# Layer one: the loads of keys, queries, values and of the RMS row stay where the program writes them on the load queue

## The chip, the cores and the metric

One core of one Trainium2 chip runs the whole kernel. The metric is the device time of one execution in microseconds (us). PE is TensorE (matmuls and transposes), DVE is VectorE, ACT is ScalarE, POOL is GpSimd; SP issues nearly all DMAs from one queue.

## What is computed

```python
scores = where(block_i >= block_j, q @ k.T / sqrt(64), -1e9)   # B=4, H=8, S=576, D=64, blocks of 64
x = softmax(scores) @ v                                        # -> 2304 tokens x 512
h = x @ w_in;  x = (h - tanh(h)) @ w_out                       # 512 -> 2048 -> 512   "layer one"
xn = x / sqrt(mean(x * x) + 1e-6) * rms_g
x = (silu(xn @ w_gate) * (xn @ w_val)) @ w_out2                # 512 -> 1536 -> 512   "layer two"
```

All in float32, each product being made of three matmuls on high and low parts.

## The kernel before

The tokens are cut into six groups of 384. **Layer one** is a loop of 96 steps, `for s in range(NSA)` (six groups times sixteen slices of the 2048 hidden columns). A step multiplies x by a slice of w_in (L776 to L778), forms h - tanh h (ACT L1038, DVE L1044, then high part `gh` on ACT L112 and low part `gl` on DVE L116) and multiplies by a slice of w_out (L809 to L811). The slices are read again for each group from DRAM copies `w1d_i` and `w1d_o` by DMAs at L745 and L755; in the first group they are made from the raw weights, which come through a ring of three staging buffers `st` (DMA L138, then ACT L149 and L151, DVE L152 and L153).

**Attention is woven into these steps.** It consists of 32 pairs, numbered p0 to p31 here (eight units of query rows, four head pairs each). A pair's keys and queries are loaded raw into `kr` and `qr`, its values into `vr` (or straight into `vp`). There are two buffers of each, so the load for pair n+2 waits until pair n has left its buffer. Pairs p4 to p11 are loaded by rows (L299, 192 KB each) and reordered by POOL at L240; pairs p12 to p31 are loaded by four DMAs each for `kr` and for `qr` in 128-byte pieces (L289), and DVE turns them by `L348 STREAM_TRANSPOSE kt<-kr` and L359 `qt<-qr`. From `kt` come the high part `kh` (ACT L112) and the low part `kl` (POOL L116), which PE multiplies (L513, L527). The probabilities `pt` go through DVE L552 or L547, ACT L554, DVE L563 and then POOL L568 or ACT L570, and PE turns them (L583); `pp` holds them turned, in high and low parts. The program calls for the loads of a pair (`load`) when it has written the preparation of the pair two places earlier.

**What sets the order.** PE's order is written by hand and is the same as the program's. In layer one the order of DVE, ACT, POOL and SP is chosen by a scheduler when the program is built, from its own simulated times; each engine then runs its list strictly in that order, and an instruction at the head of a list that waits holds up all behind it. `pin` (L102) wraps an instruction so that this scheduler may not place it ahead of the instruction which the program wrote just before it on the same engine. It adds no wait for that instruction's completion. From the start of layer two onward the lists of DVE, ACT and POOL are written by hand too.

Of the kernel before, what the change touches and what calls it, by code (L numbers as in the profile page):

```python
# [21 lines left out]
NT, DM, FF1, FF2 = 2304, 512, 2048, 1536  # L22
KD = DM // 128
TG = 384
# [79 lines left out]
def build(ctx, tc, q, k, v, w_in, w_out, w_gate, w_val, w_out2, rms_g, ident_in, out):  # L104
    nc = tc.nc
    pin = tc.keep_in_program_order
    PE, ACT, DVE, POOL, SP = nc.tensor, nc.scalar, nc.vector, nc.gpsimd, nc.sync
# [23 lines left out]
    g_bc = com.tile([128, DM], F32, name="g_bc")  # L131
# [64 lines left out]
    def first_loads():  # L196
        qn, kn, vn = (nat.tile([128, 3, H, D], F32, name=x) for x in ("qn", "kn", "vn"))

        def rows(o, src, p, eng=SP):
            for h in (2 * p, 2 * p + 1):  # L200
                eng.dma_start(out=o[:, :, h], in_=src[0, h, 0:TG, :].rearrange("(t p) d -> p t d", p=128))
        ACT.dma_start(out=ident, in_=ident_in)
        rows(kn, k, 0)
        rows(qn, q, 0, ACT)
        rows(kn, k, 1)
        rows(qn, q, 1)
        for p in range(H // 2):
            if p == 2:
                env["kq"] = kq_loads(units[1], 0)
            if p < 3:  # L210
                stage1(p)
            if p < 2:
                rows(kn, k, p + 2)
                rows(qn, q, p + 2)
            rows(vn, v, p)
        env["nat"] = (qn, kn, vn)
# [16 lines left out]
    def by_rows(u):  # L233
        return u.group in (1, 2)

    def reorder(name, src, eng):

        t = at.tile([128, S], F32, name=name, tag=name, bufs=1)
        r = src[0:96, 0:512].rearrange("p (h t d) -> p t h d", h=2, t=4)
        eng.tensor_copy(out=t[0:96, 0:512].rearrange("p (t h d) -> p t h d", h=2, t=4), in_=r)  # L240
        return t
# [43 lines left out]
    def load_kq(src, b, p, name, r0, r1):  # L285
        t = at.tile([128, S], F32, name=name, tag=name)
        for a in range(4):
            hh, dh = divmod(a, 2)
            SP.dma_start(out=t[32 * a:32 * a + 32, 0:r1 - r0].rearrange("r (t c) -> r t c", c=32),  # L289
                         in_=src[b, 2 * p + hh, r0:r1, 32 * dh:32 * dh + 32]  # L290
                         .rearrange("(t r) c -> r t c", r=32))
        return t

    def kq_loads(u, p):
        d = {}
        if by_rows(u):
            for name, src in (("kr", k), ("qr", q)):
                d[name] = at.tile([128, S], F32, name=name, tag=name)
                SP.dma_start(out=d[name][0:96, 0:512].rearrange("p (h r) -> p h r", h=2),  # L299
                             in_=src[u.b, 2 * p:2 * p + 2, 0:TG, :].rearrange("h (p t) d -> p h (t d)", t=4))  # L300
        elif u.group:
            d["kr"] = load_kq(k, u.b, p, "kr", 0, u.nk)
            d["qr"] = load_kq(q, u.b, p, "qr", u.q0, u.q1)
        return d

    def v_loads(u, p, d):
        b, W = u.b, u.nk
        if by_rows(u):
            d["kt"] = reorder("kt", d["kr"], POOL)
            d["qt"] = reorder("qt", d["qr"], POOL)  # L310
        if u.group == 0:
            d["v"] = lambda j, hh: env["nat"][2][:, j, 2 * p + hh, :]
            return
        if u.light:
            o = at.tile([128, 5, 2, 128], F32, name="vp", tag="vp")[:, :, :, 0:D]
            d["v"] = lambda j, hh: o[:, j, hh, :]
        else:
            o = d["vr"] = at.tile([128, 5, 2, D], F32, name="vr", tag="vr")
        nf, rem = divmod(W, 128)
        for hh in range(2):  # L320
            SP.dma_start(out=o[:, 0:nf, hh, :],
                         in_=v[b, 2 * p + hh, 0:nf * 128, :].rearrange("(j r) d -> r j d", r=128))
            if rem:
                SP.dma_start(out=o[0:rem, nf, hh, :], in_=v[b, 2 * p + hh, nf * 128:W, :])

    def values_prep(u, d):
        W, nb, vr = u.nk, u.nb, d["vr"]
# [47 lines left out]
    class Attn:  # L375
# [56 lines left out]
        def load(self):  # L432

            n = self.nextload
            if n < len(self.pairs):
                self.loads[n] = env.pop("kq") if n == H // 2 else kq_loads(*self.pairs[n])
            if 0 < n <= len(self.pairs):
                v_loads(*self.pairs[n - 1], self.loads[n - 1])
            self.nextload += 1
# [212 lines left out]
    with tc.manual_schedule(engines={PE.engine}):  # L652
# [339 lines left out]
        for s in range(NSA):  # L992
            g, j = divmod(s, J1)
# [21 lines left out]
                att.upto(base, goal, si / nslots)  # L1015

            if s == 8:
                SP.dma_start(out=g_bc, in_=rms_g.rearrange("(o d) -> o d", o=1).broadcast_to([128, DM]))
            if g == 0:
                conv_upto(max(2 * j + 3, EARLY + (2 * J1 - EARLY) * (2 * j + 1) // 28))  # L1020
            if 0 <= s - (J1 - 1 + KEPT - SPLIT) < 3:
# [14 lines left out]
            h = hs.pop(s)  # L1036
# [356 lines left out]
```

## Time and profile before

| what | us |
|---|---|
| median of three runs | 1009.46 (1009.27 to 1010.65) |
| the profiled execution, whole | 1010.68 |
| its span in the trace | 1008.6 |
| PE busy | 995.9 |
| DVE busy | 711.6 |
| ACT busy | 661.5 |
| POOL busy | 362.5 |

The span is the time from the first to the last instruction of the trace; the execution is 2.1 us longer. Busy times are sums over an engine's instructions, so an engine at 99% leaves little that can be removed but much that can be added.

### The profile page before, as it was taken

How to read it: one execution, taken by the hardware profiler on the slowest of the kernel's cores; microseconds unless marked ns; L12 is line 12 of the kernel's file. 1: busy time of each engine (PE TensorE's matmuls, PEld its weight loads, DVE VectorE, ACT ScalarE, POOL GpSimd, SP SyncE). 2: the span in 40 equal slices, each digit the busy share in tenths (PEclk: the TensorE clock that was granted, in tenths of full speed). 3: DMA queues.
4: the chain of work that ended last, by engine and by line, in shares of the span. 5: the costliest groups of instructions: out<-in, count | busy, mean ns of one | idle time of the engine just before them, and what ended most of it. 6: DMA issues, size and time to landing. Idle time of an engine off the chain costs nothing.

```text
span 1008.6 us, 18034 instructions
## 1 busy us (share of the span) xinstructions
PE 995.9 (99%) x5995; PEld 911.6 (90%) x5995; DVE 711.6 (71%) x1569; ACT 661.5 (66%) x1538; POOL 362.5 (36%) x538
## 2 busy tenths in 40 slices
PE   8999999999999999999999999999999999999998
PEld 5666889899988988988899889989999999999998
DVE  6878875876768676787757887966854458644565
ACT  7879988887888777788858775635732247412253
POOL 6422213332234343445334424575121470111710
PEclk9999999999999999999999999999999999999999
DMA  9899889874788699877879998987796757876664
GB/s 212 272 348 360 242 244 279 232 197 122 211 248 209 179 253 269 238 213 240 303 225 373 364 353 310 351 322 283 270 353 250 251 224 260 303 280 233 259 228 155
DMA packets 185419, 265.22 MB, mean 263 GB/s; under 512 B 109040, under 2 KB 150384, under 8 KB 178032
## 3 DMA queue, kind: packets, MB, share of 16 engines
q1 hardware_dynamic: 184240, 263.69, 80.0%
q8 instruction: 47, 0.77, 0.3%
q10 hardware_dynamic: 1088, 0.39, 0.1%
q14 instruction: 44, 0.36, 0.1%
HBM read 202.70 MB, written 61.34 MB: 262 GB/s over the span
## 4 chain that ended last, share of the span: by engine, by line
PE 81%; DVE 8%; ACT 6%; issue 2%; DMA 1%; POOL 1%; DVEq 0%; ACTq 0%; POOLq 0%
PE t L776 5%; PE gv L1126 5%; PE t L778 5%; PE t L777 5%; PE acc L809 5%; PE gv L1128 5%; PE gv L1127 5%; PE acc L811 5%; PE acc L810 5%; PE t L583 4%; PE t L513 4%; PE ga L1128 3%; PE ga L1126 3%; PE ga L1127 3%; PE ga L811 3%; PE ga L809 3%
## 5 line engine op out<-in xcount | busy, mean ns | idle before, releaser
L776 PE MATMUL t<-xh,w 128*128 128x384 f32 x384 | 138.8, 361 | 0.0
L778 PE MATMUL t<-xh,w 128*128 128x384 f32 x384 | 129.9, 338 | 0.1
L777 PE MATMUL t<-xl,w 128*128 128x384 f32 x384 | 129.2, 337 | 0.0
L1126 PE MATMUL gv<-xh,ws 128*128 128x384 f32 x330 | 110.9, 336 | 0.5 <-DVE vb L1179 0.5
L1128 PE MATMUL gv<-xh,ws 128*128 128x384 f32 x330 | 111.0, 336 | 0.2 <-DVE ws L116 0.2
L1127 PE MATMUL gv<-xl,ws 128*128 128x384 f32 x330 | 110.7, 335 | 0.0
L809 PE MATMUL acc<-w,gh 128*128 128x512 f32 x264 | 109.1, 413 | 0.4 <-ACT gh L112 0.4
L811 PE MATMUL acc<-w,gl 128*128 128x512 f32 x264 | 104.5, 396 | 0.1
L810 PE MATMUL acc<-w,gh 128*128 128x512 f32 x264 | 103.9, 394 | 0.0
L1183 POOL TENSOR_TENSOR g<-va,vb 128x384 f32<-128x384 f32 x36 | 37.4, 1038 | 162.7 <-ACT va L1182 162.7
L554 ACT ACTIVATE pt<-pt,stat 128x64 f32<-128x64 f32 (+2 forms) x144 | 81.2, 564 | 17.1 <-DVE pt L552 11.6
L776 PEld LDWEIGHTS t<-xh,w 128*128 128x128 f32 x384 | 72.2, 188 | 7.1 <-issue 3.7
L777 PEld LDWEIGHTS t<-xl,w 128*128 128x128 f32 x384 | 72.4, 189 | 1.9 <-issue 0.5
L778 PEld LDWEIGHTS t<-xh,w 128*128 128x128 f32 x384 | 72.0, 188 | 0.8 <-DVE w L116 0.8
L116 DVE TENSOR_TENSOR gl<-gt,gh 128x384 fp32r<-128x384 f32 x88 | 58.3, 663 | 20.1 <-ACT gh L112 19.6
L116 DVE TENSOR_TENSOR pp<-t,pp 128x512 fp32r<-128x512 f32 (+3 forms) x112 | 55.3, 508 | 23.3 <-ACT pp L112 22.8
L583 PE MATMUL t<-ident,pt 128*128 128x128 f32 x400 | 65.1, 274 | 3.5 <-POOL pt L568 2.0
L1044 DVE TENSOR_TENSOR gt<-t,gt 128x384 f32<-128x384 f32 x88 | 48.5, 551 | 25.3 <-ACT gt L1038 24.7
L583 PEld LDWEIGHTS t<-ident,pt 128*128 128x128 f32 x400 | 49.7, 140 | 17.5 <-POOL pt L568 5.6
L112 ACT ACTIVATE pp<-t 128x512 fp32r<-128x512 f32 (+5 forms) x144 | 60.4, 437 | 5.8 <-PE t L583 4.6
L1126 PEld LDWEIGHTS gv<-xh,ws 128*128 128x128 f32 x330 | 61.9, 188 | 1.3 <-DVE vb L1179 1.2
L1128 PEld LDWEIGHTS gv<-xh,ws 128*128 128x128 f32 x330 | 61.9, 188 | 0.6 <-DVE ws L116 0.6
(210 smaller groups left out, 2946.0 us busy)
## 6 DMA issues: line engine op xcount, KB each, us to landing
ws<-w2d SPq DMA_DIRECT2D x26, 1792.0 KB, 7.5
ws<-wod SPq DMA_DIRECT2D x21, 1536.0 KB, 6.2
w<-w1d_i SPq DMA_DIRECT2D x60, 512.0 KB, 5.0
w<-w1d_o SPq DMA_DIRECT2D x52, 512.0 KB, 5.1
w2d<-ws SPq DMA_DIRECT2D x10, 1792.0 KB, 8.4
st<-in_moe_w_out SPq DMA_DIRECT2D x28, 512.0 KB, 6.2
st<-in_moe_w_in SPq DMA_DIRECT2D x16, 512.0 KB, 6.6
w1d_i<-w SPq DMA_DIRECT2D x16, 512.0 KB, 5.7
```

Source lines behind the costliest of these rows:

```text
L116: eng.tensor_tensor(out=o, in0=full, in1=hi.bitcast(F32), op=ALU.subtract)
L554: ACT.activation(out=pt[:, 0:keys], in_=pt[:, 0:keys], func=AF.Exp, scale=-1.0, bias=least, accum_out=st[:, 8 + ti:9 + ti])
L583: PE.transpose(t[:, (j - a) * 128:(j - a + 1) * 128], pt[:, j * 128:(j + 1) * 128], ident)
L776: PE.matmul(h, lhsT=wh[:, c], rhs=xh[:, kk], start=(kk == 0), stop=False)
L777: PE.matmul(h, lhsT=wh[:, c], rhs=xl[:, kk], start=False, stop=False)
L778: PE.matmul(h, lhsT=wl[:, c], rhs=xh[:, kk], start=False, stop=(kk == KD - 1))
L809: PE.matmul(acc, lhsT=gh[:, c], rhs=wh, start=first, stop=False, skip_group_check=more)
L810: PE.matmul(acc, lhsT=gh[:, c], rhs=wl, start=False, stop=False, skip_group_check=more)
L811: PE.matmul(acc, lhsT=gl[:, c], rhs=wh, start=False, stop=last, skip_group_check=more)
L1126: PE.matmul(ps, lhsT=wh[:, c], rhs=xh[:, kk], start=(first and kk == 0), stop=False, skip_group_check=more)
L1127: PE.matmul(ps, lhsT=wh[:, c], rhs=xl[:, kk], start=False, stop=False, skip_group_check=more)
L1128: PE.matmul(ps, lhsT=wl[:, c], rhs=xh[:, kk], start=False, stop=(last and kk == nk - 1), skip_group_check=more)
```

## The change

The six `dma_start` calls of L289, L299, L321, L324 and L1018 (keys, queries, values, RMS row `g_bc`) are wrapped in `pin`. Sizes, addresses, queue and buffers stay.

```diff
@@ load_kq
-            SP.dma_start(out=t[32 * a:32 * a + 32, 0:r1 - r0].rearrange("r (t c) -> r t c", c=32),
+            pin(SP.dma_start(out=t[32 * a:32 * a + 32, 0:r1 - r0].rearrange("r (t c) -> r t c", c=32),
...
@@ kq_loads
-                SP.dma_start(out=d[name][0:96, 0:512].rearrange("p (h r) -> p h r", h=2),
+                pin(SP.dma_start(out=d[name][0:96, 0:512].rearrange("p (h r) -> p h r", h=2),
...
@@ v_loads
-            SP.dma_start(out=o[:, 0:nf, hh, :],
+            pin(SP.dma_start(out=o[:, 0:nf, hh, :],
...
-                SP.dma_start(out=o[0:rem, nf, hh, :], in_=v[b, 2 * p + hh, nf * 128:W, :])
+                pin(SP.dma_start(out=o[0:rem, nf, hh, :], in_=v[b, 2 * p + hh, nf * 128:W, :]))
...
@@ layer one, s == 8
-                SP.dma_start(out=g_bc, in_=rms_g.rearrange("(o d) -> o d", o=1).broadcast_to([128, DM]))
+                pin(SP.dma_start(out=g_bc, in_=rms_g.rearrange("(o d) -> o d", o=1).broadcast_to([128, DM])))
```

PE's list is the same in both programs. Those of SP, DVE, ACT and POOL differ from the start of layer one until the end of attention, and are the same behind it. (The numbers in the names below tell one buffer's use from the next.)

**First place: SP's list at the start.** `st_366` and `st_493` are raw weights for layer one; `kr_468`/`qr_470` and `kr_576`/`qr_578` belong to the first two pairs that are loaded by rows after the first; `vr_1214` and `vr_1491` are values, `g_bc` the RMS row. Before:

```order
L201 DMA vn_150<-in_v 128x3x64 x4
L299 DMA kr_468<-in_k 96x2x256
L299 DMA qr_470<-in_q 96x2x256
L321 DMA vp_476<-in_v 128x3x64 x2
L321 DMA vp_584<-in_v 128x3x64 x2
L321 DMA vr_1214<-in_v 128x3x64 x2
L1018 DMA g_bc_121<-in_moe2_rms_g 128x512
L321 DMA vr_1491<-in_v 128x3x64
L299 DMA kr_576<-in_k 96x2x256
L321 DMA vr_1491<-in_v 128x3x64
L138 DMA st_366<-in_moe_w_out 128x1024
L299 DMA qr_578<-in_q 96x2x256
```

And after:

```order
L201 DMA vn_150<-in_v 128x3x64 x4
L138 DMA st_366<-in_moe_w_out 128x1024
L299 DMA kr_468<-in_k 96x2x256
L299 DMA qr_470<-in_q 96x2x256
L321 DMA vp_476<-in_v 128x3x64 x2
L710 DMA w1d_i_0_85<-w100_356 128x1024
L138 DMA st_493<-in_moe_w_in 128x4x256
L299 DMA kr_576<-in_k 96x2x256
L299 DMA qr_578<-in_q 96x2x256
L321 DMA vp_584<-in_v 128x3x64 x2
```

The raw weights have moved ahead of `kr_468`; the values for later pairs and `g_bc` (five DMAs) have gone from this place to ones far behind it.

**Second place: SP's list around the keys of pair p27, `kr_5197`.** The rows L745 and L755 are weight slices of layer one. Before:

```order
L745 DMA w103_4774<-w1d_i_11_96 128x1024
L289 DMA kr_5197<-in_k 32x18x32 x4
L745 DMA w102_4841<-w1d_i_10_95 128x1024
L828 DMA x2d_63<-x2s_4715 128x512
L745 DMA w101_4910<-w1d_i_9_94 128x1024
L828 DMA x2d_63<-x2s_4761 128x512
L828 DMA x2d_63<-x2s_4769 128x512
L289 DMA qr_5202<-in_q 32x6x32 x4
L755 DMA w113_4776<-w1d_o_11_112 128x1024
```

And after:

```order
L755 DMA w113_5066<-w1d_o_7_108 128x1024
L890 DMA wod_84<-wc_5126 128x3x256 x2
L745 DMA w100_5285<-w1d_i_4_89 128x1024
L755 DMA w112_5137<-w1d_o_6_107 128x1024
L289 DMA kr_5197<-in_k 32x18x32 x4
L289 DMA qr_5202<-in_q 32x6x32 x4
L745 DMA w103_5364<-w1d_i_3_88 128x1024
L755 DMA w111_5235<-w1d_o_5_106 128x1024
```

The keys stood between slices 11 and 10 of a group and stand now between slices 4 and 3 of it, with the queries right behind them.

**Third place: DVE's list around the transposes of the same pair.** Before:

```order
L116 TENSOR_TENSOR gl_5093<-gt_5089,gh_5092 128x384
L348 STREAM_TRANSPOSE kt_5451<-kr_5197 128x576
L116 TENSOR_TENSOR pp_5068<-t_5139,pp_5068 128x4x128
L563 RECIPROCAL stat_4956<-stat_4956 128x3
```

And after:

```order
L116 TENSOR_TENSOR gl_5254<-gt_5250,gh_5253 128x384
L613 TENSOR_TENSOR avt_5275<-t_5268,avt_5275 64x384
L348 STREAM_TRANSPOSE kt_5451<-kr_5197 128x576
L359 STREAM_TRANSPOSE qt_5480<-qr_5202 128x192
L116 TENSOR_TENSOR wc_5359<-fu_4469,wc_5359 128x1024
L613 TENSOR_TENSOR avt_5295<-t_5289,avt_5295 64x384
L116 TENSOR_TENSOR pp_5308<-t_5309,pp_5308 128x4x128
```

`kt_5451` has moved fourteen rows back in the list, behind two more slices' `gl`, and both transposes now stand together.

## Rows read from the trace of the kernel before

**Rows 1.** The head of the page: span; busy time and instructions of each engine.

```profile
span 1008.6 us, 18034 instructions
PE 995.9 (99%) x5995; PEld 911.6 (90%) x5995; DVE 711.6 (71%) x1569; ACT 661.5 (66%) x1538; POOL 362.5 (36%) x538
```

**Rows 2.** Busy time by stretch: PE, PEld, DVE, ACT, POOL; PE clock, DMA share, GB/s.

```profile
0.00:40.00 40.00, 35.79 (x222) 24.62 (x224) 30.48 (x118) 29.82 (x103) 25.73 (x68) 1.00 0.93 234
40.00:100.00 60.00, 58.74 (x284) 41.56 (x285) 47.90 (x112) 52.46 (x130) 14.02 (x29) 1.00 1.00 339
100.00:500.00 400.00, 398.33 (x2295) 355.72 (x2294) 296.57 (x752) 328.44 (x795) 142.77 (x254) 1.00 0.81 231
```

**Rows 3.** PE's waits over the whole span: us in total, times, longest us.

```profile
PE t L583 <- POOL pt L568: 2.0, 3, 1.3
...
PE t L583 <- DVE xs L623: 0.9, 1, 0.9
...
PE t L583 <- DVE gt L1044: 0.5, 1, 0.5
...
PE t L527 <- DVE pp L116: 0.3, 1, 0.3
```

**Rows 4.** DMA issues of the whole span: times, KB each, median us from issue to landing.

```profile
kr<-in_k SPq DMA_DIRECT2D x64, 72.0 KB, 4.5
...
qr<-in_q SPq DMA_DIRECT2D x64, 24.0 KB, 3.5
```

**Rows 5.** Line L348: its instructions (ns min/median/max), and all that DVE waited for.

```profile
L348 DVE STREAM_TRANSPOSE kt<-kr x20: 536/769/779, 145.1 to 447.5; 128x576 f32<-128x576 f32 x16, 128x384 f32<-128x384 f32 x4
...
  POOL kl L116: 2.5, 3
```

**Rows 6.** SP's timeline at the start: start us, us, instruction.

```profile
16.96 1.56 SPq L299 DMA_DIRECT2D kr<-in_k  x1
...
24.36 0.48 SPq L1018 DMA_DIRECT2D g_bc<-in_moe_rms_g  x1
...
26.99 0.38 SPq L299 DMA_DIRECT2D qr<-in_q  x1
```

**Rows 7.** Line L299 from 26.9 to 27.3 us, one load: from issue to landing.

```profile
DMA to landing us min/median/max: 6.4/6.4/6.4
```

**Rows 8.** POOL's timeline at the start: start, us, instruction, idle time ahead in brackets.

```profile
33.53 0.61 POOL L240 COPY qt<-qr 96x512 f32<-96x512 f32 x1 [3.26 <-PE t L513]
```

**Rows 9.** The chain of waits from 30 to 66 us: start us, us, what.

```profile
34.12 0.65 POOL pt L568
...
54.59 6.30 DMA st<-in_moe_w_out
```

**Rows 10.** SP's timeline around 384 us, one row.

```profile
384.44 0.44 SPq L755 DMA_DIRECT2D w<-w1d_o  x1
```

**Rows 11.** Line L289 from 95 to 480 us: issues (ns min/median/max), and issue to landing.

```profile
L289 SPq DMA_DIRECT2D kr<-in_k x80: 312/491/2447, 103.1 to 414.4; - x80
...
DMA to landing us min/median/max: 1.6/3.8/7.4
```

**Rows 12.** DVE's timeline from 376 to 394 us.

```profile
376.66 0.77 DVE L348 STREAM_TRANSPOSE kt<-kr 128x576 f32<-128x576 f32 x1
...
385.37 0.55 DVE L613 TENSOR_TENSOR avt<-t,avt 64x384 f32<-64x384 f32 x1
388.16 1.75 DVE L116 TENSOR_TENSOR wc<-fu,wc 128x1024 fp32r<-128x1024 f32 x1 [2.25 <-ACT wc L864]
...
392.59 0.78 DVE L348 STREAM_TRANSPOSE kt<-kr 128x576 f32<-128x576 f32 x1 [0.34 <-POOL kl L116]
...
393.73 0.68 DVE L116 TENSOR_TENSOR pp<-t,pp 128x512 fp32r<-128x512 f32 x1
```

**Rows 13.** PE's timeline, one row: the first matmul into the bank that this pp empties.

```profile
396.93 0.50 PE L527 MATMUL t<-kh,qp 64*128 64x512 f32 x2
```

**Rows 14.** The chain of waits from 100 to 480 us, one row.

```profile
376.74 0.69 DVE kt L348
```

More of the change, by code (lines that the diff above doesn't have):

```diff
@@ L288, in load_kq @@
             hh, dh = divmod(a, 2)
-            SP.dma_start(out=t[32 * a:32 * a + 32, 0:r1 - r0].rearrange("r (t c) -> r t c", c=32),
-                         in_=src[b, 2 * p + hh, r0:r1, 32 * dh:32 * dh + 32]
-                         .rearrange("(t r) c -> r t c", r=32))
+            pin(SP.dma_start(out=t[32 * a:32 * a + 32, 0:r1 - r0].rearrange("r (t c) -> r t c", c=32),
+                             in_=src[b, 2 * p + hh, r0:r1, 32 * dh:32 * dh + 32]
+                             .rearrange("(t r) c -> r t c", r=32)))
         return t
@@ L298, in kq_loads @@
                 d[name] = at.tile([128, S], F32, name=name, tag=name)
-                SP.dma_start(out=d[name][0:96, 0:512].rearrange("p (h r) -> p h r", h=2),
-                             in_=src[u.b, 2 * p:2 * p + 2, 0:TG, :].rearrange("h (p t) d -> p h (t d)", t=4))
+                pin(SP.dma_start(out=d[name][0:96, 0:512].rearrange("p (h r) -> p h r", h=2),
+                                 in_=src[u.b, 2 * p:2 * p + 2, 0:TG, :].rearrange("h (p t) d -> p h (t d)", t=4)))
         elif u.group:
@@ L320, in v_loads @@
         for hh in range(2):
-            SP.dma_start(out=o[:, 0:nf, hh, :],
-                         in_=v[b, 2 * p + hh, 0:nf * 128, :].rearrange("(j r) d -> r j d", r=128))
+            pin(SP.dma_start(out=o[:, 0:nf, hh, :],
+                             in_=v[b, 2 * p + hh, 0:nf * 128, :].rearrange("(j r) d -> r j d", r=128)))
             if rem:
-                SP.dma_start(out=o[0:rem, nf, hh, :], in_=v[b, 2 * p + hh, nf * 128:W, :])
+                pin(SP.dma_start(out=o[0:rem, nf, hh, :], in_=v[b, 2 * p + hh, nf * 128:W, :]))
     def values_prep(u, d):
```

## The prediction, written before the changed kernel was run

> **What bounds the kernel now.** I read the head of the page first. PE is busy for 995.9 of 1008.6 us [rows 1], so a change that leaves PE's list as it is can only add to or take from the 12.7 us in which PE idles. The busy time by stretch says where these lie: 4.2 us in the first 40 us, 1.3 from 40 to 100, and 1.7 in the 400 us in which attention and layer one run together [rows 2]. The lists behind attention do not change. So the change can win back at most about 7 us, part of which is the start that no load list shortens; 3 us (the middle two stretches) and the one start-up wait below are what is really in reach. What it can lose has no such bound. PE's waits name the releasers: POOL L568 for 2.0 us in three waits, all of them at the start, then single waits of 0.9, 0.5 and 0.3 us on DVE [rows 3]. No wait of PE in the middle names a DMA. Last I looked at L348, since its `kr` is what the change delays: in 20 transposes DVE idled ahead of them only for POOL, 2.5 us in three waits, and never for the load [rows 5].
>
> **The change, part by part.** `pin` adds no instruction and no byte. It moves DMAs on SP, and the scheduler rearranges DVE, ACT and POOL around them.
>
> *1. The start, gain.* POOL's copy `qt<-qr` at 33.53 us stood idle for 3.26 us [rows 8]. The row names PE, but the load that it reads was issued at 26.99 [rows 6] and took 6.4 us [rows 7], so it landed at 33.4: the load came last. Behind the copy in POOL's list stands L568 [rows 9], and behind that the longest of PE's waits on it, 1.3 us [rows 3]. In the new list five DMAs that stood ahead of this load are gone (four of 96 KB of values and the RMS row of 256 KB, 640 KB). At the 234 GB/s of this stretch [rows 2] they are 2.7 us of transfer. That is more than the 1.3 us that PE waited, so I take a gain of 1.3 us; bounds 0 and 1.3.
>
> *2. The start, loss.* 512 KB of raw weights now go ahead of `kr_468`, which was issued at 16.96 [rows 6]. By the same rate it lands 2.2 us later. No row tells how much of that PE would see; bounds 0 and 2.2, and I take 0.5, near the lower end, since the copies that need it are followed by 1.5 us and more of POOL idling in the same stretch (POOL is busy 25.7 of 40 us [rows 2]). What the raw weights gain by going first is bounded by the chain's one long DMA step there, 6.3 us for an `st` [rows 9]; PE idles only 1.3 us from 40 to 100, so this can return 0 to 1.3 us. I take nothing.
>
> *3. The middle, loss: DVE stands in front of the load.* Pair p27 shows it. Before, `kt<-kr` ran at 376.66 [rows 12], with its keys long there. In the new list the keys follow the load of `w112_5137`, which is the one at 384.44 [rows 10]. The four issues take 0.49 us each [rows 11], the last at 384.88 + 3 x 0.49 = 386.35, and land 4.5 us after it [rows 4], at 390.9. DVE comes to the transpose behind `avt`, which ends at 385.37 + 0.55 = 385.92 [rows 12]. It waits 4.9 us. After 0.77 for the transpose it is 391.6; the queries, issued behind the keys (last at 388.2, 3.5 us to landing [rows 4]), are there at 391.7, and 0.38 us later, at 392.1, DVE comes to `wc`, which ran at 388.16. Ahead of `wc` DVE had idled for 2.25 us anyway, which is counted in this: the list is 3.9 us late. What that costs PE: the row `pp` at 393.73 comes 3.9 us later, less the 0.78 + 0.34 of the next pair's transpose and its wait, which no longer stands ahead of it [rows 12]: at 396.5, ending at 397.2. PE's L527 writes into the bank that this empties at 396.93 [rows 13], so PE waits 0.3 us there. Other rows of that piece have less to spare: followed along the dependencies to the next matmul that needs them, I read 0.8 us where this one has 2.5, and that gives 2.0. I take 1.2 us for p27.
>
> I went through the other 19 transposes in the same way, with the new place in SP's list, 4.5 us to landing, and the new place in DVE's list. Seven (p27 among them) come out with DVE waiting 1.7 us or more, about 16 us in all; eight with 0.2 to 1.1 us, 4 us in all; five with none. DVE is busy 297 of 400 us here [rows 2], so a wait is soon made good, and DVE can slip by 0.9 to 3 us before PE notices. The eight small ones cost nothing. The six other large ones leave 0 to 1 us each; I take 0.4, so 2.4 us, and with p27 3.6. The bounds are 0 (all is covered) and 16 - 7 x 0.9 = 9.7 us (the least cover everywhere). I take a value in the lower half, nearer to the reckoned row than to the sum with least cover.
>
> What would cover go to? A late `kt` makes `kh` (ACT) and `kl` (POOL) late as well, but PE wants them later still: the L527 at 396.93 [rows 13] is still that of p26, and comes 6 us after the keys of p27 land by the reckoning above. So the loads alone are not late for PE; only what stands behind them in DVE's list is.
>
> *4. The middle, gain by the new order.* Where the transpose moves away from a tight spot, it frees it. The chain of waits has `kt` L348 in it at 376.74 for 0.69 us [rows 14], just ahead of the wait of 0.3 us that PE has on `pp` [rows 3]. I count 0.3. The waits of 0.9 and 0.5 us [rows 3] may vanish or grow with any new order; bounds plus and minus 1.4, taken as 0.
>
> *5. Stores and weight slices on SP.* The loads now come in one piece of 8 to 12 issues, 0.49 us each [rows 11], so up to 5 us in which no slice of w_in or w_out is issued. No wait of PE in the middle is put down to a slice [rows 3], and the slices are read three steps ahead. I count 0, bounds 0 and 1.
>
> The sum: -1.3 + 0.5 + 3.6 - 0.3 = +2.5 us. The profiled execution took 1010.68 us, 1.2 over the median of the three runs (1009.46). On the median's side that is 1012.0 us.
>
> The Trainium skill, DMA: Bandwidth & Descriptors, in its section Anatomy of one DMA, gives for a DMA of GpSimd's path a fixed 2.0 us plus the bytes at 436 GB/s. For 72 KB that would be an estimate of 2.2 us, where the row on this kernel's SP path has 4.5 [rows 4]. By the page's figure DVE would wait 2.3 us less at each large pair and step 3 would come to about zero, the sum to -0.9 us. I keep to the row.
>
> **The rivals.** *Quick landings or full cover: no change.* If the new, emptier queue lets the loads land near the shortest of 1.6 us [rows 11] rather than at 4.5, each of the seven waits shrinks by 2.9 us, from 16 to about 2 in all, and nothing reaches PE. Or the cover is just wider than I read. Then the steps 1, 2 and 4 are left: 1009.5 - 1.1 = 1008.4 us, within the limit. For it speaks that DVE idles a quarter of the time; against it that DVE's list runs strictly in order and some places have under 1 us.
>
> *Faster.* The start gains its 1.3 us, the staging ring passes on its 1.3, step 2 costs nothing, and the new order loses PE's waits in the middle (1.7): up to 4.3 us, 1005.2; I would expect 1006.5. For it speaks that 1.4 MB (the 640 KB of step 1 and 768 KB of keys and queries of p8 and p9) leave the stretches in which the DMA engines are busiest, at 0.93 and 1.00 [rows 2]. Against it, PE's waits of 40 us onward name engines and no load.
>
> *Much slower.* The cover is at its least everywhere, and the waits feed each other, since a late DVE makes PE late, PE frees the slices' buffers late, and SP, in order, issues the next keys later still. It decides from the point where a wait of DVE exceeds 0.9 us at most pairs: +9.7 + 0.5 - 1.6 = 1018 us.
>
> *It does not do what it says.* That would be an SP list unchanged, and the lists show otherwise: no chance given.
>
> **How the numbers follow.** A measurement of this kernel tells a difference of about 0.2%, 2 us, from no change. Slightly slower, +2 to +6 us: 0.35. Much slower, above +6: 0.08. Within 2 us: 0.30. Faster by over 2 us: 0.27. My forecast of 1012.0 stands close to the limit, so part of its chance is in the middle case already. The slower cases hold 0.43, the likeliest single one from 1011.5 to 1015.5. The range for 8 in 10 reaches down to 1006, most of the faster case, and up to 1017, most of the way to the much slower one.
>
> **What would show it.** Right: L348 of the new trace idles on a DMA `kr<-in_k`, some 10 to 20 us in all, with five to ten waits over 1.5 us; PE's waits between 100 and 500 us grow from 1.7 to about 5 us, on DVE `pp`, `pt` or `gt`; the wait of 1.3 us on POOL L568 is gone, and `qt<-qr` is copied about 1 to 3 us earlier. Wrong: L348 idles on DMA and PE's idle time in this stretch stays at 1.7 (cover was wider); L348 does not idle on it (landings were quicker); or PE's waits grow on ACT or on slices `w` (step 5). If the time drops under 1007.5, the start or the staging ring held more than PE's waits show.

## The result: 1.5% slower

The changed kernel takes 1023.68 us (median of five runs, 1023.18 to 1027.89) against 1009.46 before: a ratio of 1.0148, with a 95% interval of 1.0135 to 1.0161. Its profiled execution took 1023.68 us as well, with a span of 1021.8. The direction was forecast and the size was not: +14.2 us where +2.5 was predicted, outside the range.

The head of its page, then the busy time by stretch (PE, PEld, DVE, ACT, POOL; PE clock, DMA share, GB/s), which answer to [rows 1] and [rows 2]:

```profile
span 1021.8 us, 17998 instructions
PE 1000.4 (98%) x5995; PEld 913.7 (89%) x5995; DVE 715.6 (70%) x1569; ACT 659.5 (65%) x1538; POOL 363.3 (36%) x538
```

```profile
0.00:40.00 40.00, 37.10 (x232) 25.60 (x232) 30.25 (x118) 30.04 (x104) 23.59 (x67) 1.00 0.85 215
40.00:100.00 60.00, 58.18 (x277) 41.40 (x275) 48.20 (x109) 51.12 (x125) 17.04 (x33) 1.00 0.96 323
100.00:500.00 400.00, 389.32 (x2218) 345.04 (x2217) 290.70 (x734) 315.02 (x771) 136.96 (x246) 1.00 0.76 224
```

PE idles 2.9 us in the first 40 (4.2 before), and 10.7 us from 100 to 500 (1.7 before). So in these two traces the start is better and the middle much worse. Since PE's list is the same, the start of each matmul can be compared in the two traces, and the delay read off as it builds up (worked out from these starts):

| matmul starts, before | after | delay |
|---|---|---|
| 20.12 | 20.44 | +0.3 |
| 34.81 | 33.66 | -1.2 |
| 100.09 | 99.77 | -0.3 |
| 180.12 | 181.03 | +0.9 |
| 240.05 | 244.95 | +4.9 |
| 300.00 | 306.81 | +6.8 |
| 340.10 | 351.12 | +11.0 |
| 440.13 | 452.50 | +12.4 |
| 500.05 | 513.60 | +13.5 |
| 1000.02 | 1013.15 | +13.1 |

From 100 to 500 us PE loses 13.8 us; behind attention nothing is added and 0.4 us is given back. Where the loss comes from is shown by lines L348 and L359 of the changed kernel (first the transposes of keys, then those of queries; under each what DVE waited for: us, times):

```profile
L348 DVE STREAM_TRANSPOSE kt<-kr x20: 578/778/779, 159.1 to 474.8; 128x576 f32<-128x576 f32 x16, 128x384 f32<-128x384 f32 x4
...
  DMA kr<-in_k: 18.3, 14
  DMA qr<-in_q: 2.7, 1
```

```profile
L359 DVE STREAM_TRANSPOSE qt<-qr x20: 357/378/581, 160.4 to 475.9; 128x192 f32<-128x192 f32 x16, 128x384 f32<-128x384 f32 x4
...
  DMA qr<-in_q: 7.3, 9
```

Before, DVE never waited for a load there [rows 5]. Now it waits 28.3 us in 24 places. PE's waits (us in total, times, longest) have moved from POOL to what stands behind these transposes on DVE, where [rows 3] had 0.3 us on `pp`:

```profile
PE t L776 <- DVE gt L1044: 2.7, 2, 1.4
PE t L619 <- DVE pp L116: 2.2, 1, 2.2
PE t L527 <- DVE pp L116: 1.8, 2, 1.0
PE t L513 <- DVE pp L116: 1.5, 1, 1.5
```

How a load reaches PE stands in the chain of waits from 200 to 240 us (start us, us, what), around the loads of p16:

```profile
209.93 0.47 SPq L289
210.44 0.47 SPq L289
210.96 0.47 SPq L289
211.47 2.72 DMA qr<-in_q
...
214.31 0.59 DVE qt L359
214.92 0.52 ACT qh L112
215.47 0.52 ACT qh L112
216.01 0.87 ACT pt L554 x2
216.88 0.49 ACT pp L112
217.40 0.69 DVE pp L116
```

SP issues the eight loads of a pair one after the other, about 0.5 us each, the last one lands, DVE turns the queries, ACT splits them twice, and only then does ACT's list come to `pt` and `pp`, for which DVE and then PE wait. The late transpose is therefore passed on through two lists, DVE's and ACT's. At this one place, with 1.1 us of DVE waits (0.41 at L348 and 0.73 at L359), PE lost 2.4 us. They are not p16's alone: DVE had waited another 1.5 us for the loads of p15 only 8 us earlier.

The chain has a way back too, ahead of the loads of p17:

```profile
224.05 0.67 DVE w L116
224.74 0.32 SPq L751
225.11 0.42 SPq L289
```

In the new list these loads stand behind a store of layer one (L751), which waits for what DVE writes at L116, so here a late DVE makes the next loads late. SP idled ahead of L751 for DVE's `w` for 18.6 us in five places, against 2.1 us in two before.

At the start, POOL's timeline shows what the prediction expected, against [rows 8]:

```profile
31.22 0.61 POOL L240 COPY qt<-qr 96x512 f32<-96x512 f32 x1 [0.25 <-DMA qr<-in_q]
```

The copy comes 2.3 us earlier, and the matmul behind it gains 1.5 us between one start and the next. That the change brought this is not shown; e1 and x9 below speak against it.

### The profile page after: what moved, and what is told of

It is laid out like the page before. It is cut to its first block, busy times and chain, and to the rows that moved or that the text cites. A ratio compares the mean times of both kernels' runs of the same rounds, so it can differ in the third digit from the quotient of the medians.

```text
span 1021.8 us, 17998 instructions
## 1 busy us (share of the span) xinstructions
PE 1000.4 (98%) x5995; PEld 913.7 (89%) x5995; DVE 715.6 (70%) x1569; ACT 659.5 (65%) x1538; POOL 363.3 (36%) x538
## 4 chain that ended last, share of the span: by engine, by line
PE 61%; DVE 12%; ACT 11%; DMA 6%; SPq 4%; issue 4%; POOL 1%; DVEq 0%; ACTq 0%; POOLq 0%
PE gv L1126 5%; PE gv L1128 5%; PE gv L1127 5%; SPq L289 4%; PE acc L809 3%; PE t L776 3%; PE acc L811 3%; PE acc L810 3%; PE t L778 3%; PE t L777 3%; PE ga L1128 3%; PE ga L1126 3%; PE ga L1127 3%; PE ga L811 2%; PE ga L809 2%
## 5 line engine op out<-in xcount | busy, mean ns | idle before, releaser
L116 DVE TENSOR_TENSOR pp<-t,pp 128x512 fp32r<-128x512 f32 (+3 forms) x112 | 55.6, 510 | 23.5 <-ACT pp L112 22.9
L116 DVE TENSOR_TENSOR gl<-gt,gh 128x384 fp32r<-128x384 f32 x88 | 57.9, 658 | 19.2 <-ACT gh L112 19.0
L112 ACT ACTIVATE gh<-gt 128x384 fp32r<-128x384 f32 x88 | 45.8, 520 | 31.0 <-DVE gt L1044 30.5
L1126 PEld LDWEIGHTS gv<-xh,ws 128*128 128x128 f32 x330 | 61.9, 188 | 1.3 <-DVE vb L1179 1.1
```

What stands on the lines that cost most here:

```text
L112: return ACT.activation(out=o, in_=i, func=AF.Copy)
L116: eng.tensor_tensor(out=o, in0=full, in1=hi.bitcast(F32), op=ALU.subtract)
L1126: PE.matmul(ps, lhsT=wh[:, c], rhs=xh[:, kk], start=(first and kk == 0), stop=False, skip_group_check=more)
```

## The experiments

**Theory A**: DVE, which runs its list in order, stands in front of loads that land just behind it, and PE pays. **Theory B**: the scheduler's new lists for DVE, ACT and POOL cost time by themselves. **Theory C** came up with the result: A holds, but the time by which DVE may slip is smaller than the prediction reckoned.

The kernels named x hold the lists fixed. Each instruction of DVE, ACT, POOL and SP gets the edge that `pin` adds (issue order, no wait), from its predecessor in a table; so the lists are the changed kernel's row by row, except for what is said. Differences in time are against the kernel before on the same chip in the same series.

**One part alone.** First the change without L289, then L289 alone (the change wraps five calls in all, not six):

```diff
@@ e2_rest_only: load_kq as before, the other four calls pinned
-            pin(SP.dma_start(out=t[32 * a:32 * a + 32, 0:r1 - r0].rearrange("r (t c) -> r t c", c=32),
+            SP.dma_start(out=t[32 * a:32 * a + 32, 0:r1 - r0].rearrange("r (t c) -> r t c", c=32),
```

> The change for L299, L321, L324 and L1018 alone; the loads of L289 (keys and queries of p12 to p31) stay free for the scheduler. Theory A: L348 does not wait for its loads, as before; the start gains its 1.3 us; the time is 1007.5 to 1010 us. Theory B (any new order costs): DVE's list differs from the one before in 54 rows instead of 245, so part of the loss stays, 1011 to 1018 us.

> The change for L289 alone (keys and queries of p12 to p31); L299, L321, L324 and L1018 stay free. Theory A: the whole loss of the middle is here, without the gain of the start, 1020 to 1026 us. If the loads of values and of the RMS row carry part of the loss: 1012 to 1018 us.

The first took 1009.43 us against 1009.98, ratio 0.9995 (0.9986 to 1.0005): no change, and L348 waits for no load. The second took 1026.09 against 1009.77, ratio 1.0161 (1.0146 to 1.0176), just above its range, with 29.2 us of DVE waits on loads at the two lines. So the whole loss is in the loads of keys and queries of p12 to p31.

The gain of 1.5 us at 34 us appears in both; in the first it is used up by 53 us (+1.5 us at one matmul there). But the lists of e1 are those of the kernel before up to 105 us, and x9 below, which has the lists of before throughout, shows the gain as well. POOL's copy in x9:

```profile
31.79 0.61 POOL L240 COPY qt<-qr 96x512 f32<-96x512 f32 x1 [1.81 <-PE t L637]
```

In e1 it is at 32.07. Both issue its load at 25.5 us, where the profiled execution of before, which took 1.2 us more than the median, issued it at 26.99 [rows 6]. So the wait of 1.3 us at 34 us was that execution's own. At 100 us PE stands 0.3 us ahead of the trace of before in e1 and 0.9 in x9; in the kernels with all of the changed lists there it stands between 0.3 us behind and 2.1 us ahead, so one trace cannot tell what the start gains or loses. By e2's time the changes of the start are worth nothing that can be measured.

**The loads alone, earlier or later.** The lists of PE, DVE, ACT and POOL are the changed kernel's; on SP's list the eight loads of each pair pass one or three weight slices forward, or one back (17 pairs). For p27 three forward is:

```diff
@@ x1_three_earlier, SP
+L289 DMA kr_5197<-in_k 32x18x32 x4
+L289 DMA qr_5202<-in_q 32x6x32 x4
 L755 DMA w113_5066<-w1d_o_7_108 128x1024
 L890 DMA wod_84<-wc_5126 128x3x256 x2
 L745 DMA w100_5285<-w1d_i_4_89 128x1024
 L755 DMA w112_5137<-w1d_o_6_107 128x1024
-L289 DMA kr_5197<-in_k 32x18x32 x4
-L289 DMA qr_5202<-in_q 32x6x32 x4
```

> As the kernel with three slices, but the loads pass one slice only, some 2.6 us. Theory A: of the waits at L348 only what exceeds 2.6 us is left (0.9, 0.2 and 0.1 us at three pairs), some 1 to 3 us in all with landings that vary, and the time is 1008 to 1013 us. Theory B: 1020 to 1025 us.

> The changed kernel with its lists of PE, DVE, ACT and POOL held fixed row by row; only on SP's list each pair's eight loads of keys and queries (p12 to p31) stand ahead of the three weight slices that they stood behind, so they are issued some 7 us earlier. Theory A (DVE waits at L348 and L359 for loads that land too late, and PE pays for it): DVE's waits on those DMAs, 18.3 us at L348 in the changed kernel, fall below 2 us, PE's idle time from 100 to 500 us goes from 10.7 to under 4 us, and the time is 1008 to 1011 us, the gain of 1.1 us at the start included. Theory B (the new order of DVE, ACT and POOL costs PE, and the waits are covered): the time stays within 1020 to 1025 us, whatever the waits do.

> All lists as in the changed kernel, but on SP's list the loads of 17 of the 20 pairs (not p15, p24, p29) stand one weight slice further back, some 2.6 us. Theory A: DVE waits about 2.6 us longer at 16 to 17 pairs, some 40 us more in all; with the cover of about 1 us a pair that the changed kernel has used up already, 25 to 42 us of it reach PE: 1048 to 1066 us. Theory B: under 1030 us.

| kernel | DVE's waits on loads, us | time, us | before | ratio (95%) |
|---|---|---|---|---|
| x3, one later | 103.8 | 1118.73 | 1009.98 | 1.1076 (1.1051 to 1.1101) |
| changed kernel | 28.3 | 1023.68 | 1009.46 | 1.0148 (1.0135 to 1.0161) |
| x2, one earlier | 7.0 | 1011.72 | 1009.98 | 1.0018 (1.0008 to 1.0027) |
| x1, three earlier | 0 | 1019.17 | 1009.98 | 1.0085 (1.0070 to 1.0100) |

One slice forward takes back 12 us with the new lists of the other engines in place. That settles A against B. The waits left in x2 are more than the 1 to 3 us expected; its time is in the range. One slice back costs another 95 us, where 24 to 42 more were expected. The trace fits a feedback: SP idles 41.9 us ahead of L755 and 32.8 ahead of L745 for PE to free the slices' buffers, and 27.3 ahead of L751 for DVE (35.9, 25.2 and 18.6 in the changed kernel), and the next loads stand behind these. No run breaks that loop, and part of the 95 us goes with a lower granted clock (last section).

The three slices forward missed both forecasts. No transpose waits any more (L348 and L359 show no wait on a DMA), and yet PE lost 8.7 us at one place, 218 to 228 us: 4.8 us in one wait, and 0.32 x 10 = 3.2 us by the granted clock, which was 0.68 in these 10 us. PE's and SP's timelines of that kernel:

```profile
218.09 0.66 PE L776 MATMUL t<-xh,w 128*128 128x384 f32 x1 [4.84 <-DMA w<-w1d_i]
```

```profile
204.60 2.88 SPq L289 DMA_DIRECT2D qr<-in_q  x4
209.22 1.85 SPq L289 DMA_DIRECT2D kr<-in_k  x4
211.16 1.95 SPq L289 DMA_DIRECT2D qr<-in_q  x4
213.21 0.41 SPq L745 DMA_DIRECT2D w<-w1d_i  x1
```

The keys of p18 wait at the head of SP's list until p16's have been turned (DVE comes to that at 208.6), and the slice of w_in behind them goes out at 213.21, too late for the matmul at 218. So SP's list has the same trouble in reverse: a load that is too early for its buffer holds up the slices. In x2 the same slice is issued at 222.34, and PE's wait of 2.5 us at 226.86 is the only large one left. The trace names DVE's `ql` for it, but the slice landed at 226.72, just before that matmul.

**Loads fitted to both sides.**

> All lists as in the changed kernel, but on SP's list the loads of p13, p20, p21, p27 and p29 pass two weight slices forward, those of p18 none and the other 14 pairs' one. In the kernel where all pass one slice, PE's only large wait left (2.5 us at 226.9 us) comes with a w_in slice that was issued at 222.3 us behind p18's loads, which had waited on SP for their buffers; where all pass three, PE waits 4.8 us for a slice at the same place. Theory A with this SP term: that wait is gone, DVE's waits on loads are under 5 us, and the time is 1007.5 to 1010 us. If the wait at 227 us came from the order of DVE instead: 1010.5 to 1012.5 us.

It took 1008.54 us against 1009.77, ratio 0.9989 (0.9980 to 0.9999). L348 waits for no load, L359 as follows (us, times), and PE's wait at 227 us is gone; so that wait came from SP's list:

```profile
  DMA qr<-in_q: 2.6, 2
```

This is the fastest kernel of the study, 1.2 us under the kernel before, with an interval that just excludes no change. It has the new lists of DVE, ACT and POOL in full, so these cost nothing by themselves.

**The reader moved, not the load.** In the changed kernel both transposes are pinned too, which sets them 15 to 25 rows back in DVE's list:

```diff
@@ e3_turn_pinned
-            DVE.transpose(kt[:, 0:W], kr[:, 0:W])
+            pin(DVE.transpose(kt[:, 0:W], kr[:, 0:W]))
...
-            DVE.transpose(qt[:, 0:nq], qr[:, 0:nq])
+            pin(DVE.transpose(qt[:, 0:nq], qr[:, 0:nq]))
```

> The changed kernel with the two transposes of DVE (L348, L359) pinned as well, which puts them 15 to 25 rows later in DVE's list, behind the landing of their loads; the loads stay where the change put them. Theory A: DVE does not wait for the loads (under 2 us in all); the loss of the middle goes, 1007.5 to 1012 us, unless keys turned that late make PE wait for them directly. Theory B (new orders cost): 1016 to 1026 us, since the lists differ from the ones before in more rows still (333 against 245 on DVE).

It took 1020.85 us against 1009.77, ratio 1.0112 (1.0097 to 1.0127). DVE waits for no load, but PE's timeline now has the direct wait of which the expectation warned; its other large waits, of 0.8 to 1.9 us, are on DVE's `pp` and `avt`:

```profile
190.66 0.79 PE L527 MATMUL t<-kh,qp 64*128 64x512 f32 x2 [3.14 <-ACT qp L112]
```

The queries of p13 had landed at 172.3 us and were turned at 188.8. Theory B's range holds this time too, but the trace shows what the time is made of, and x5 has excluded B. The run says that the transposes can't simply be put off: the place where they stand is bounded from both sides.

**How much each wait costs.** Two kernels ask which of the waits PE pays for.

> All lists as in the changed kernel, but the loads of only the seven pairs that the prediction reckoned to wait 1.7 us or more (p12, p13, p21, p22, p23, p27, p29) pass one weight slice forward on SP's list. Theory A as the prediction sized it (the seven large waits carry all of the loss, the others are covered): 1010 to 1013.5 us, as where all 20 pairs pass one slice (1011.7). Theory C (cover is thinner than reckoned, so waits of 0.3 to 1.6 us at the other pairs reach PE too, for which the steps of PE's delay at 213 and 233 us speak): half of the loss stays, 1015 to 1019.5 us.

It took 1017.85 us against 1009.77, ratio 1.0083 (1.0066 to 1.0100). With the seven pairs helped, 19.1 us of waits are left, and 8.1 us of loss. PE's delay still grows by 1.3 us at 214 and 1.2 us at 234 us, beside the pairs p16 to p18, which were not helped and whose waits are 0.3 to 1.6 us, and by 1.9 us at 382, behind p26. (There DVE idled 2.0 us more, put down to POOL, though the last of p26's keys landed only 0.1 us before its transpose; so 19.1 is the least that the waits can be.) Of the seven, p13 and p21 still wait 2.1 and 1.7 us, but PE's delay does not grow at p13 and grows by 0.5 us at p21. So the pairs that the prediction had called covered carry about half of the loss: theory C.

Then the slip alone, with no DMA moved: the transposes of keys are done two or three times, one behind the other, all lists fixed, on the lists of the fitted kernel (x7, x8) and on those of the kernel before (x9).

```diff
@@ x7_twice
-            DVE.transpose(kt[:, 0:W], kr[:, 0:W])
+            DVE.transpose(kt[:, 0:W], kr[:, 0:W])
+            DVE.transpose(kt[:, 0:W], kr[:, 0:W])
```

> The lists of the fitted kernel (1008.5 us, no waits on loads), with every transpose of keys (L348) done twice, one behind the other: 0.77 us more (0.57 at four pairs) of DVE at 20 places, 14.6 us in all, and no wait for any DMA. It measures by itself how much DVE can slip there. The cover that the prediction reckoned (0.9 us at the least): nothing reaches PE, 1008 to 1010 us. Theory C (thin cover): 4 to 8 us reach it, 1012.5 to 1017 us.

> As the kernel with two, each transpose of keys three times: 1.5 us more at 20 places, 29 us in all, which is what the loads cost DVE in the changed kernel (28 us), evenly spread. The prediction's cover: 0 to 4 us reach PE, 1008.5 to 1013 us. Theory C: half or more, 1020 to 1030 us.

> The lists of the kernel before, row by row, with each transpose of keys three times: 29 us more of DVE at the places where the transposes stood before. The prediction read its cover from this trace. By it 0 to 6 us reach PE, 1010 to 1016 us. If it read the cover wrongly and not only the new places: 1020 to 1030 us.

| kernel | DVE work added at 20 places, us | time, us | before | ratio (95%) | loss, us, against the same lists |
|---|---|---|---|---|---|
| x7, fitted lists | 14.6 | 1011.43 | 1010.17 | 1.0015 (1.0005 to 1.0024) | 2.5 |
| x8, fitted lists | 29.2 | 1021.12 | 1010.17 | 1.0109 (1.0094 to 1.0124) | 12.2 |
| x9, lists before | 29.2 | 1031.98 | 1010.17 | 1.0217 (1.0201 to 1.0233) | 21.8 |

The last column is each kernel's difference from before, less that of the kernel with the same lists and single transposes (-1.2 for the fitted one, 0 for before). On average DVE can slip by 0.73 us a pair at a price of 0.13 each; the next 0.73 us cost 0.49 each. In the order of before, 1.46 us a pair cost 1.1 each. x8 came out as theory C said; x7 fell between the two ranges, with 1.8 of its 2.5 us at one matmul (327 us), and x9 2 us above its upper one. The waits of PE in x9 name the places (us in total, times, longest):

```profile
PE t L527 <- DVE pp L116: 6.6, 5, 1.9
PE t L776 <- DVE pp L116: 2.1, 4, 0.9
```

29 us of evenly spread transposes (x8) cost 12.2 us, nearly what 28 us of waits did in the changed kernel (14.2), while DVE waits for loads for 0.8 us only. So a slip of DVE by itself is enough for such a loss.

**The time to landing.**

```diff
@@ x4_contig: each partition reads one run of the same size
-                         in_=src[b, 2 * p + hh, r0:r1, 32 * dh:32 * dh + 32]
-                         .rearrange("(t r) c -> r t c", r=32))
+                         in_=src[b, 2 * p + hh, r0:r1, :].rearrange("(r t) d -> r t d", r=64)[32 * dh:32 * dh + 32]
+                         .rearrange("r t d -> r (t d)").rearrange("r (t c) -> r t c", c=32))
```

> The changed kernel, all lists the same; the loads of L289 read the same number of bytes as whole runs (2304 bytes a partition for keys) in place of 128-byte pieces, so PE works on keys and queries in another arrangement (the scores are not those of the reference); everything else is as in the changed kernel. It tells what the time to landing is worth. Theory A: if these land 1.5 to 2.5 us sooner than the 4.1 us of the changed kernel, DVE's waits on loads fall from 28 to 6 to 14 us and the time to 1011 to 1018 us. If the landing is set by the busy DMA engines and not by the pieces: 1021 to 1025 us.

It took 1012.35 us against 1010.17, ratio 1.0024 (1.0013 to 1.0036). The DMA issues of the two kernels (times, KB each, median us from issue to landing), first the changed kernel, then x4:

```profile
kr<-in_k SPq DMA_DIRECT2D x64, 72.0 KB, 4.3
...
qr<-in_q SPq DMA_DIRECT2D x64, 24.0 KB, 2.0
```

```profile
kr<-in_k SPq DMA_DIRECT2D x64, 72.0 KB, 3.7
...
qr<-in_q SPq DMA_DIRECT2D x64, 24.0 KB, 2.6
```

The median for keys falls by 0.6 us only, less than expected, and that for the small queries does not fall. The waits fall from 28.3 to 17.9 us, not as far as the 6 to 14 expected, while the time is in its range; p16 and p23 no longer wait at all, while p12, p13, p20, p21, p27, p29 and p30 keep 1.4 to 2.9 us each at L348. 17.9 us here cost 2.2 us, and 19.1 us in x6 cost 8.1, so it matters more which pairs wait than how long all wait together. That the pairs left here are those with more to spare is read from this comparison; no run tested it pair by pair.

## Why the prediction was right or wrong

- **Step 1, the gain at the start: the agreement is luck.** PE gained 1.5 us at that matmul (1.3 predicted), but e1 and x9 gain it with the lists of before: the wait belonged to the one profiled execution and not to the lists. The bytes were counted in part only, too. By the two lists, `w1d_i_0` and `st_493`, 512 KB each, also moved ahead of the queries, and the two `vp_584`, 96 KB each, behind them; so more bytes than before go ahead of this load, not 640 KB fewer.
- **Step 2, the loss at the start: not decided.** PE was 0.3 us late before 34 us, for 0.5, and 0.3 us early at 100 us, where -0.8 was the net of both steps. The traces of the same lists differ by more than that at 100 us.
- **Step 3, DVE in front of the loads: mechanism right, the sum of the waits right, the loss wrong by a factor of four. This is the step that failed.** The waits at L348 were put at 20 us and measured 21.0, in part by luck: the seven large pairs had 11.4 us for 16, the others 9.6 for 4. (p27: 4.9 reckoned, 0.6 measured, since its first load was issued 5.3 us before DVE came to the transpose, and not 1.0.) The term "seven large ones, 0 to 1 us each beyond the cover, the eight small ones nothing", 3.6 us, measured 13.8. Three things stood in its place. First, cover: it was read as 0.9 to 3 us a pair in the trace of before; x9 shows that the lists of before had less, 1.46 us a pair costing 1.1, and x7 and x8 that the new ones take up about 0.6 of the first 0.73 us a pair and 0.24 of the next. Second, the small waits: by x6 the pairs outside the seven carry about half. Third, L359: its waits on queries, 7.3 us, come 1 to 3 us behind those at L348 and add to them, and they were left out of the sum. The error had a common root. The text said that only what stands behind the transposes in DVE's list would be late. The chain at 209 to 217 us shows ACT's list in between: `qh` waits there for the transpose of the queries, and `pt` and `pp` stand behind it. For `kh` alone ACT's idle time on L348 is 7.2 us, in six waits. How much of the 13.8 us each of the three makes up is not shown.
- **Step 4, the wait at 378 us: wrong.** `kt` did leave that spot, but PE's wait on `pp` there grew from 0.3 to 0.8 us (the 1.8 us above, less the 1.0 us of the longer one at 218). In x1, x2 and x5, which have the same lists but for SP's and whose loads come earlier, it is gone; so the new order did free it, and the late loads took that back.
- **Step 5, slices behind the burst of loads: right for this change**, where no large wait of PE names a slice. x1 shows the price, 4.8 us at one matmul, when the loads stand where their buffer is still in use. For such a place a bound of 1 us is too low.
- **The rivals.** "Much slower" was the case that came, given 0.08, and 1018 us was still too low, as its sum counted only the seven pairs' waits less 0.9 us each. x3 fits its feedback over SP, which no run isolates. "Quick landings" did not come about: the median for keys was 4.3 us, against 4.5 before. That for queries, which step 3 took as 3.5, did fall, to 2.0. The Trainium skill, DMA: Bandwidth & Descriptors, Specifications, gives 512 bytes as the least transfer for line rate. x4 agrees in direction for keys, whose runs grow from 128 to 2304 bytes (0.6 us sooner), but not for queries, whose runs are 768 bytes (0.6 us later); most of the landing time stays.

One more part of the loss was not in the sum at all. Behind PE's longest wait, 2.2 us up to 335.5, PE's granted clock fell for a while (columns as in the stretches above):

```profile
330.00:335.00 5.00, 3.34 (x19) 2.58 (x18) 4.89 (x10) 2.93 (x8) 2.54 (x3) 1.00 0.71 195
335.00:340.00 5.00, 4.50 (x17) 4.06 (x18) 3.51 (x12) 4.55 (x11) 0.47 (x2) 0.67 0.86 159
340.00:345.00 5.00, 5.00 (x29) 4.55 (x28) 3.15 (x6) 3.49 (x7) 2.78 (x3) 0.99 0.27 60
```

A granted clock of 0.67 over 5 us means that some two thirds of it ran at the lower level, 1.2 GHz, and costs 0.33 x 5 = 1.65 us. PE's waits of 1.2 to 1.5 us at 172, 238 and 303 us were not followed by this. In the other kernels the clock fell behind waits of 1.9 us (x9, 393 us), 2.2 (x6, 382) and 2.3 (e1, 389), but not behind 2.3 us near the same place in x8, nor behind 2.5 us in x2. What decides between them stays open here. Over the matmuls of the middle PE's idle time grows from 1.7 to 11.0 us, 9.3 of the 13.8 us lost; with the 1.65 some 2.9 us are left that the rows do not tell apart.

## What to carry to other kernels

A load that is kept from running ahead cost nothing by itself here (x5); what costs is an engine that runs its list in order and has the load's reader standing just ahead of the landing, so read the landing against the reader's place in that list, pair by pair. Do not take the slack from the reader's own list alone: follow the late result into the next engine's list and see what stands behind it there, or measure it by doing the reader's work twice. The right place for a load has two sides, since too early it waits on the queue for its buffer and holds up what stands behind it. And before a wait in one trace is put down to the program, see whether a second execution of the same lists has it.

## What the runs showed that was not expected

- The same 29 us of extra DVE work cost 12.2 us on one set of lists and 21.8 us on another, though PE's list is the same in both and DVE idles a quarter of the time before the extra work: the spare time of an engine says little about its cover.
- Shifting 17 groups of loads by one slice on SP cost 95 us on top of the changed kernel, and from 100 to 520 us the granted clock fell to 0.90 there, which is up to 0.10 x 420 = 42 us of the 95:

```profile
100.00:520.00 420.00, 357.56 (x1877) 313.43 (x1875) 240.88 (x621) 267.84 (x665) 110.95 (x198) 0.90 0.61 178
```
